# An S4 convolution and gated MLP on one core: the opening's pole tables, w_mod and x loads, and the reads of x at the convolution's end

## Chip, cores and metric

The kernel runs on one core of a Trainium2 chip. The metric is the device time of one execution in microseconds (us), as the median over runs. PE is TensorE's matmul stream, DVE is VectorE, ACT is ScalarE, POOL is GpSimd, SP is SyncE; SP and POOL issue most DMAs, each from a queue of its own.

## The reference

x is 2048 positions by 576 channels, split by the kernel into 16 blocks of 128 positions.

```python
mod = (silu(c) @ w_mod).reshape(1, 6, 1, -1)     # sa, ca, ga, sb, cb, gb; w_mod is 576 x 3456
h = layernorm(x) * (1 + ca) + sa
# S4: dt = exp(log_dt); K[d,l] = Re sum_n C[d,n] exp(dt (A_re + i A_im) l) dt B[d,n]
x = x + ga * (causal_conv(h, K) + h * Dskip)      # by rfft/irfft of length 4096
h = layernorm(x) * (1 + cb) + sb
z = gelu(h @ w_in)                                # 576 x 4608
g = w_sp @ layernorm(z[..., 2304:]) + b_sp        # w_sp is 2048 x 2048
out = x + gb * ((z[..., :2304] * g) @ w_out)
```

## The kernel before

**Stages.** The first stage builds the convolution's kernel K for 36 groups of 16 channels, layer-normalises x, and convolves; it ends with the first MLP operations near 385 us of the profile. The rest is the MLP. The change touches the first stage, and the loads for the MLP that this stage starts.

**The opening.** `poles` turns log_dt, A and B*C (576 x 128 poles) into three tables: the real exponent and log weight (`al`, `lw`), the turns of one and of 64 positions (`tau`, `tau64`), and a phase `ph`. It runs as p0 for the first quarter of the channels (tiles 128x144) and as p1 for the other three (128x432). `split3` cuts each table into three bf16 parts (copy on ScalarE, subtract on VectorE, twice), which GpSimd's queue writes to DRAM (`pa_d`, `pb_d`, rows of 288 bytes). `poles_load` reads them back, turned, as `lb`, `lc` and `la`; from there TensorE with `sel` makes exponents and angles. A unit e copies and exponentiates the exponents into a tile `et` (ScalarE), a unit t takes sine and cosine into `ft` (VectorE rounds, ScalarE evaluates), a unit p multiplies both (VectorE, tiles `pg`, 1024 wide) and k and 1 contract them on TensorE.

**Modulation and normalisation.** `mod_load` brings one sixth of w_mod (two tiles of 648 KB; tiles `wm`, or for k=0,1 the buffers named k_a and k_b, which hold K later). `mod_unit` multiplies it by silu(c) on TensorE into psum tiles `pk`, copies them to `mpart` (ScalarE), sums over partitions, and makes `gar` (from 2), `cga` (from 1) and `sga` (from 0). `ln_load` brings four blocks of x (1152 KB), `ln_stats` takes mean and variance: with two passes of ScalarE for the first two fours, with VectorE's batch-norm statistics for the rest. `ln_rows` scales a block by `cga` (VectorE) and makes a small row tile `rt`.

**The convolution's end.** Units u, z and v transform and multiply; v is copied from psum by ScalarE and written to DRAM (`v_d`) by GpSimd's queue. `y_vload` reads v_d in another layout, `y_xload` a block of x, a unit y adds both on TensorE and ScalarE or VectorE and stores x1. Steps L are the MLP's start: loads of w_in quarters into `wst` (L0: the third, 1.31 MB), their sums of squares on ScalarE (`start_sum`), scales, and the high and low f16 parts (`start_hi`, `start_lo`) into `wz`. Then the first rows of x1 are normalised (`xz`, `n`), transposed (`pt`, `nt`) and multiplied (`pz`).

**What sets the order.** ORDER is a list written out by hand: each token runs the next piece of one unit, and engines execute in that program order. O and P are p0 and p1, M, S, R, A are mod_unit, ln_stats, ln_rows, ln_half; w and i load w_mod on SyncE's or GpSimd's queue, x and j load x, r, g and a load r1t, Q is poles_load. PLAN lists, for each ring of buffers, which buffer each new tile takes; buffer letters (et_a, pk_b) are those of the ring. Nearly every instruction is recorded at the helper's line 224.

Of the kernel before, what the change touches and what calls it, by code (L numbers as in the profile page):

```python
# [18 lines left out]
D = 576  # L19
# [13 lines left out]
    "et": "0123401232013423014021304123024104120",  # L33
# [21 lines left out]
B0 O0 O0 O0 O0 B2 O0 O0 O0 O0 B7 O0 B1 O0 O0 O0 B6 O0 O0 O0 O0 O0 O0 x0 O0 O0 O0 O0 P0 S0 O0 S0 B3 O0 O0 i2 O0 O0 O0 P0 M2 O0 O0 S0 S0 B4 P0 S0 O0 Q0 P0 e1 S0 M2 e1 i1 e0  # L55
P0 P0 g0 e1 e0 P0 e0 e1 P0 t1 t2 i0 g1 O0 M2 e0 P0 M1 t1 t2 t1 P0 P0 t0 w3 P0 M1 t0 M2 t1 t0 t2 M1 M0 M1 M0 t0 e2 j1 R1 P0 p1 M3 t2 M0 p1 M3 R0 e2 R3 e6 p1 M0 B5 e2 M0 e6
M3 w4 k1 e4 e2 P0 M3 k1 O0 P0 e3 11 p0 e4 11 e6 M4 M0 e5 p0 P0 p0 e6 S1 S1 p2 M4 k0 M4 p2 11 R2 p2 e5 k0 e5 S1 M0 M3 M0 P0 k2 M4 e5 M0 P0 t5 k2 A0 e3 A0 S1 A0 A0 A0 w5 t5
S1 e3 P0 e3 A0 t3 S1 A1 t5 A1 A1 r2 A1 P0 t3 R4 A1 t7 A0 R5 A1 A2 A2 O0 P0 t3 t3 A2 A2 t4 P0 A1 A2 A2 A3 p3 A2 A3 t5 P0 r3 A3 A3 t4 t4 j2 M4 10 10 e4 A3 A3 A3 e4 12 p3 12
e7 p3 e7 P0 e7 R7 t7 10 R6 P0 p5 S2 12 k3 e8 e7 O0 k3 e8 A4 S2 A4 S2 A4 e8 S2 A4 A4 A4 e8 p5 P0 A5 t4 A5 A5 P0 A5 p5 A5 p4 A5 t7 a4 A4 A5 t6 A6 A6 A6 p4 A6 t6 A6 p4 A6 t8
A7 A7 P0 t7 A7 A7 O0 k4 A6 P0 S2 A7 13 t6 p7 A7 k4 t8 p7 R9 14 13 O0 k5 P0 P0 a5 t6 14 14 t8 p7 Q1 13 t8 M5 x3 k7 P0 e11 R8 A7 k5 M5 S3 k7 S3 A8 A8 e11 R11 e9 A8 e10 e11  # L60
P0 e9 e11 P0 p6 S3 S3 A8 P0 A8 R10 t10 A8 e10 A9 t10 A9 A9 A9 p8 p8 r6 e10 A9 A9 t9 e10 t10 A10 A8 P0 A10 A10 A10 A9 t11 p6 A10 A10 17 P0 t10 M5 p6 17 k6 M5 p8 t11 t9 17
k6 A11 A11 r7 S3 t11 t11 e12 A11 A11 Q2 15 R13 A11 A11 A10 p11 k8 t9 15 15 R12 A11 k8 A12 p11 A12 e12 A12 p11 A12 e14 A12 t14 A12 A13 e14 p10 A13 t14 A13 R15 e9 p10 A13
p10 A13 R14 A13 e9 t14 A12 e12 t12 e12 A14 A14 t9 A14 t15 A14 A14 t12 A13 t14 A14 t12 A15 A15 t14 O0 O0 A15 e16 k10 P0 A15 P0 A15 16 A15 P0 O0 p9 t12 k11 16 M5 p9 A14 A15
p9 C0 16 t14 18 c1 k10 f0 18 110 k11 18 110 e14 U2 110 U1 U0 t15 p12 111 t15 111 z2 111 t15 u2 t16 p12 u2 U5 p12 u0 e14 k9 c0 z2 z2 u0 k9 t16 k12 U4 p14 u1 19 U14 t16 U7
e16 k12 e15 19 t16 19 U23 e13 e15 e15 e16 u1 e15 c3 u7 e16 e13 p14 u4 u7 e13 u4 p14 c2 p15 z1 z1 e13 t13 U29 v2 u14 U6 t16 v2 p15 z4 U10 u14 t13 u6 t13 p15 t18 k15 z4 u6
u5 t16 k15 z1 p16 t18 p16 u29 e18 u5 U15 v1 z0 t13 u29 t18 e17 X1 t18 v1 U3 e18 115 115 u10 v1 v2 z0 u10 z0 X3 p16 e17 115 k14 k14 u3 b1 e17 e22 u3 p13 U12 e22 t17 e17
# [20 lines left out]
def consts():  # L87
# [53 lines left out]
    rgt = np.zeros((6, 8, 8, 32))  # L141
    rge = np.zeros((6, 8, 8, 32))
    rpe = np.zeros((6, 8, 8, 64))
    rgt[:3] = eye[None, :, :, None] * a
    rgt[3:] = eye[None, :, :, None]
    rge[:3] = eye[None, :, :, None] * (64 * a)
    rge[3:] = eye[None, :, :, None]
# [89 lines left out]
def ssm(tc, I, x1_d, consts_s, dram, mod_d, mlp):  # L237
# [6 lines left out]
    with ExitStack() as ctx:  # L244
# [26 lines left out]


        def poles(c0, c1, Q, own=None):
            w = 144 * (c1 - c0)
            f0, f1 = CW * c0, CW * c1

            def t(n, dt=F32):
# [2190 lines left out]
```

## Time and profile before

| | |
|---|---|
| three runs | 1690.81, 1693.52, 1693.48 us; median 1693.48 |
| profiled execution's own time | 1691.0 us |
| its span | 1688.9 us |
| busy PE / DVE / ACT / POOL | 1615.6 / 1298.4 / 873.8 / 209.7 us |
| 200 to 300 us, busy PE / DVE / ACT | 96.98 / 97.85 / 95.52 us |
| first p unit (pg_a) | 51.29 us |
| last y unit's matmuls end, first transposes of n begin | 383.85, 384.32 us |
| granted TensorE clock | 0.99 |

A row of the timeline gives start, duration, engine, line, operation, out<-in, shape and count; the bracket at its end is the idle time just before it, with what ended that. In tables by window the columns are busy time and instructions of each engine, then clock, share of the 16 DMA engines and GB/s.

### The profile page before, as it was taken

The numbers are of one execution on the slowest core, as the hardware profiler recorded it, in microseconds if no ns is written. First come the engines' busy times: TensorE is split into PE (matmuls) and PEld (weight loads), VectorE is DVE, ScalarE is ACT, GpSimd is POOL, SyncE is SP. The second block draws the span as 40 slices with busy tenths as digits, with TensorE's granted clock in tenths as the row PEclk, the third lists the DMA queues.
The fourth block names the chain that finished last, engine by engine and source line by source line (L and its number), as shares of the span: only waits on it lengthen the run. The fifth ranks groups of instructions, "written<-read, shape, count | busy, mean of one in ns | idle before, by whom it ended". The sixth has DMA issues, their size and how long they took to land.

```text
span 1688.9 us, 39922 instructions
## 1 busy us (share of the span) xinstructions
PE 1615.6 (96%) x16868; PEld 1235.7 (73%) x16868; DVE 1298.4 (77%) x2241; ACT 873.8 (52%) x1307; POOL 209.7 (12%) x340
## 2 busy tenths in 40 slices
PE   3778999989999999999999999999999999999999
PEld 1344677755555557778878888888888888888887
DVE  7898999867989877988997776894443487787555
ACT  6889999675776664555444433342321133353221
POOL 3251111112222110000000000000111100111100
PEclk9978999999999999999999999999999999999999
DMA  9667645596888898776738887664667573777560
GB/s 231 170 215 229 203 140 176 171 317 208 280 287 243 251 261 297 242 270 234 249 118 302 282 292 257 219 218 166 232 213 243 189 221 121 275 281 252 189 241 29
DMA packets 186402, 380.61 MB, mean 225 GB/s; under 512 B 38464, under 2 KB 105792, under 8 KB 185456
## 3 DMA queue, kind: packets, MB, share of 16 engines
q1 hardware_dynamic: 145216, 182.10, 35.2%
q0 software_dynamic: 34528, 169.11, 30.1%
q10 hardware_dynamic: 6480, 26.86, 3.9%
q8 instruction: 132, 2.16, 0.5%
q14 instruction: 46, 0.38, 0.1%
HBM read 272.73 MB, written 105.29 MB: 224 GB/s over the span
## 4 chain that ended last, share of the span: by engine, by line
PE 77%; DVE 7%; DMA 3%; issue 2%; ACT 2%; SPq 0%; POOL 0%; ACTq 0%; DVEq 0%; POOLq 0%
PE ps L224 58%; PE pz L224 10%; PE pk_b L224 2%; PE pk_a L224 2%; DMA zset<-set_d 2%; PE pk_c L224 2%; PE pk_d L224 1%; DVE zset L224 1%; DVE gt L224 1%; DVE bsz L224 1%; PE ps_a L224 0%; PE ps_b L224 0%; DMA v_d<-v_a 0%; PE pt L224 0%; DMA uu_a<-in_x 0%
## 5 line engine op out<-in xcount | busy, mean ns | idle before, releaser
L224 PEld LDWEIGHTS <-zset 128*128 128x128 f16 x7182 | 702.2, 98 | 86.5 <-DMA zset<-set_d 2.0
L224 PE MATMUL ps<-wsp,zset 128*128 128x256 f16 x6048 | 666.8, 273 | 2.2 <-DMA zset<-set_d 1.1
L224 PE MATMUL pz<-wz,nt 128*128 128x512 f16 (+1 forms) x1120 | 220.8, 358 | 1.5 <-ACT nt L224 1.0
L224 ACT ACTIVATE z<-gt 128x1024 f16<-128x1024 f32 x56 | 59.0, 1054 | 250.4 <-DVE gt L224 250.4
L224 PEld LDWEIGHTS <-nt 128*128 128x128 f16 x1120 | 109.4, 98 | 107.1 <-ACT nt L224 1.5
L2164 POOL DMA_DIRECT2D zset<-set_d x96 | 50.8, 529 | 862.5 <-PE ps L224 619.7
L224 PE MATMUL ps<-wout,z 128*128 128x288 f16 x1092 | 138.4, 286 | 0.0
L224 DVE SCALAR_TENSOR_TENSOR gt<-ps,sc,bsp 128x512 f32<-128x512 f32 x36 | 27.0, 749 | 143.0 <-PE ps L224 141.3
L224 PEld LDWEIGHTS <-z 128*128 128x128 f16 x1176 | 115.1, 98 | 28.9
L224 DVE TENSOR_TENSOR raw<-raw 128x256 f32<-128x256 f32 (+3 forms) x238 | 126.8, 539 | 7.7 <-DMA raw<-z_d 3.5
L224 PE MATMUL ps<-n2o,zset 128*128 128x256 f16 x1134 | 128.2, 273 | 0.0
L224 DVE SCALAR_TENSOR_TENSOR gt<-ps,sc,gt 128x512 f32<-128x512 f32 (+1 forms) x180 | 122.2, 696 | 7.6
L224 ACT ACTIVATE zset<-raw 128x1792 f16<-128x1792 f32 x48 | 81.1, 1691 | 59.3 <-PE ps L224 21.6
L224 DVE TENSOR_TENSOR zset<-raw,zset 128x1792 f16<-128x1792 f32 x48 | 96.9, 2020 | 15.7 <-ACT zset L224 15.7
L224 DVE TENSOR_TENSOR z<-ps,z 128x512 f32<-128x512 f32 (+1 forms) x126 | 72.0, 599 | 32.3 <-ACT z L224 25.9
L224 ACT ACTIVATE z<-pz,sc 128x512 f32<-128x512 f32 (+1 forms) x96 | 51.9, 574 | 39.9 <-PE pz L224 32.7
L224 ACT ACTIVATE wsp<-raw,sc 128x1792 f16<-128x1792 f32 x25 | 44.5, 1783 | 46.2 <-DVE raw L224 40.2
L224 ACT ACTIVATE z<-z,sc 128x1024 f32<-128x1024 f32 x21 | 24.1, 1148 | 76.0 <-DVE z L224 72.3
L224 ACT ACTIVATE z1b<-gt 128x512 f16<-128x512 f32 (+1 forms) x22 | 17.7, 821 | 84.0 <-DVE gt L224 84.0
L224 PE MATMUL ps<-n2q,wf 128*128 128x512 f16 x252 | 55.7, 379 | 0.0
L224 DVE BATCH_NORM_STATS2 bsz<-z 128x6 f32<-128x384 f32 x96 | 48.4, 548 | 5.0 <-ACT z L224 4.4
L224 DVE SCALAR_TENSOR_TENSOR wsp<-raw,sc,wsp 128x1792 f16<-128x1792 f32 x25 | 52.0, 2078 | 0.3 <-ACT wsp L224 0.3
(793 smaller groups left out, 2772.0 us busy)
## 6 DMA issues: line engine op xcount, KB each, us to landing
zset<-set_d POOLq DMA_DIRECT2D x96, 896.0 KB, 5.2
raw<-z_d SPq DMA_DIRECT2D x48, 512.0 KB, 5.6
set_d<-zset ACTq DMA_DIRECT2D x24, 896.0 KB, 6.4
z_d<-z POOLq DMA_DIRECT2D x32, 576.0 KB, 8.2
zset<-wa_d POOLq DMA_DIRECT2D x18, 896.0 KB, 4.9
raw<-in_w_spT SPq DMA_DIRECT2D x25, 512.0 KB, 4.4
set_d<-zset SPq DMA_DIRECT2D x12, 896.0 KB, 5.8
wst<-in_w_in SPq DMA_DIRECT2D x8, 1024.0 KB, 9.3
```

Source lines behind the costliest of these rows:

```text
L224: return self.tc.keep_in_program_order(f(*a, **k))
L2164: self.nc.gpsimd.dma_start(o, self.set_d[f, j - 1] if j else self.wa_d[f])
```

## The change

- **Pole tables.** `poles` returns ten separate chains that ORDER steps one by one. The four products of B and C are one instruction, both absolute values one, `tau64` needs no multiplication (the factor 64 stands in a constant), the angle takes 8 operations where it took 13, and `split3` works on two tables at once. All parts go to one DRAM tensor `p_d`. A_re is loaded last. p0's tiles lie in two buffers of the et ring.
- **Loads.** w_mod 2, 1, 0, r1t 0 and 1, and x blocks 4 to 7 are issued by SyncE right behind `small`. GpSimd's queue keeps the pole tables; the two memsets of `lb` run first.
- **Statistics.** The second four blocks of x use VectorE's batch-norm statistics. `rt` is made for two blocks at once.
- **The convolution's end.** A tile `xl` holds x blocks 8 to 15 for channels 384 to 575; it is loaded with `x1l` (now four blocks) at step D, and three loads of x in steps X fall away. The third quarter of w_in is loaded ahead of some dozen other loads of SyncE that it stood behind, into the unused half of a k1 buffer and a new tile `wrow`; its sum of squares is two instructions, and the sum of the fourth quarter moves behind the last v copies. Step L14 moves behind a piece of y9, and the last y pieces change places.

Some of the code (`...` marks what is left out; the rest of ORDER and PLAN is in the rows below):

```diff
-        def poles(c0, c1, Q, own=None):
+        def poles(c0, c1, Q, order, own=None):
...
-                V.tensor_tensor(wr, Cr, Br, op=ALU.mult)
-                V.tensor_tensor(wi, Ci, Br, op=ALU.mult)
-                V.tensor_tensor(q1, Ci, Bi, op=ALU.mult)
...
+                V.tensor_tensor(s(10, 4).rearrange("p (b c f) -> p b c f", b=2, c=2), bc(sm(6, 2)[:, None], shape), bc(sm(8, 2)[:, :, None], shape), op=ALU.mult)
...
+            def split3(i, m, row, at):
...
+                A.activation(pt[:, :, 0], src, AF.Copy)
+                yield
+                V.tensor_tensor(q, src, pt[:, :, 0], op=ALU.subtract)
...
+            return [step(), turns(), weights(), log(), ratio(), second(), angle(),
+                    split3(1, 2, 6, 0), split3(3, 2, 0, 2), split3(5, 1, 12, 4)]
...
-            if i < 2:
+            if i < 1:
...
-            elif c == NC - 1:
-                xb = mlp.x1l[:, 4 * q - 4:4 * q]
+            elif (c, q) == (NC - 1, 1):
+                xb = mlp.x1l
+            elif c >= NC - 2 and q > 1:
+                xb = mlp.xl[:, 4 * q - 8:4 * q - 4, CH0[c] - 384:CH0[c] - 384 + CHW[c]]
...
-        self.x1l = wzp.tile([128, 12, CHL], F32, name="x1l")
-        S.dma_start(self.x1l, I["x"][:, 4:, D - CHL:])
+        self.x1l = wzp.tile([128, 4, CHL], F32, name="x1l")
+        S.dma_start(self.x1l, I["x"][:, 4:8, D - CHL:])
+        self.xl = wzp.tile([128, 8, D - 384], F32, name="xl")
+        S.dma_start(self.xl, I["x"][:, 8:, 384:])
...
+    def start_early(self, q, pool, t):
+        self.wts[q] = t, pool.tile([128, 512], F32, name="wrow", bufs=1)
+        self.win_parts(*self.wts[q], FH + 512 * q, 512)
```

GpSimd's queue in the opening, before: pole writes, a load of w_mod among them, then the three reads and more loads.

```order
L224 DMA pb_d<-pt 64x3x144 x2
L224 DMA pa_d<-pt 64x3x144 x4
L224 DMA pb_d<-pt 64x3x144 x2
L224 DMA wm<-in_w_mod 96x1728 x2
L224 DMA pa_d<-pt 64x3x144 x2
L224 MEMSET lb 32x1152
L224 DMA lb<-pb_d 48x1152 x2
L224 DMA lc<-pa_d 48x1152 x2
L224 DMA la<-pa_d 48x1152 x2
L224 DMA k_a<-in_w_mod 96x1728 x2
```

The same queue after the change.

```order
L223 MEMSET lb_124 32x1152
L223 MEMSET lb_126 32x1152
L223 DMA p_d<-pt 64x6x144 x2
L223 DMA lc<-p_d 48x1152 x2
L223 DMA p_d<-pt 64x6x144 x2
L223 DMA p_d<-pt 64x3x144 x2
L223 DMA lb_124<-p_d 48x1152 x2
L223 DMA la<-p_d 48x1152 x2
L223 DMA p_d<-pt 64x6x144 x12
```

The read of `lc` moved ahead of the writes of (`al`, `lw`) and of `ph`; the loads of w_mod left this queue.

VectorE on p0's weights B*C, before: from the first product to the multiplication by the reciprocal.

```order
L224 TENSOR_TENSOR t_wr<-et_a 128x144
L224 TENSOR_TENSOR t_wi<-et_a 128x144
L224 TENSOR_TENSOR t_q_126<-et_a 128x144
L224 TENSOR_TENSOR t_wr<-t_wr,t_q_126 128x144
L224 TENSOR_TENSOR t_q_127<-et_a 128x144
L224 TENSOR_TENSOR t_wi<-t_wi,t_q_127 128x144
L224 TENSOR_SCALAR et_a<-t_wr 128x144
L224 TENSOR_SCALAR et_a<-t_wi 128x144
L224 TENSOR_TENSOR et_a<-et_a 128x144 x2
L224 TENSOR_SCALAR et_a<-et_a 128x144
L224 RECIPROCAL t_rnd<-et_a 128x144
L224 TENSOR_TENSOR et_a<-et_a,t_rnd 128x144
```

The same place after; the second row is the first subtraction of `split3`, the three of `ec` belong to silu(c).

```order
L223 TENSOR_TENSOR et_e<-et_a 128x576
L223 TENSOR_TENSOR et_e<-et_a,pt 128x288
L223 TENSOR_SCALAR ec<-ec 96x6
L223 RECIPROCAL ec<-ec 96x6
L223 TENSOR_TENSOR ec<-ec,cT 96x6
L223 TENSOR_TENSOR et_e<-et_e 128x144 x2
L223 TENSOR_SCALAR et_a<-et_e 128x288
L223 SCALAR_TENSOR_TENSOR et_a<-et_a 128x144
L223 TENSOR_TENSOR et_a<-et_a 128x144
L223 RECIPROCAL et_e<-et_a 128x144
L223 TENSOR_TENSOR et_a<-et_a,et_e 128x144
```

Thirteen instructions of the weights became eight, of up to four times the width.

ScalarE near 350 us, before: the last copies of v (to v_a and v_b) around the sums of squares of the third and fourth quarters of w_in.

```order
L224 ACTIVATE v_a<-pk_d 128x256
L224 ACTIVATE v_a<-pk_b 128x256
L224 ACTIVATE wz,acc<-wst 128x5x512 x2
L224 ACTIVATE v_b<-pk_d 128x256
L224 ACTIVATE v_b<-pk_b 128x256
L224 ACTIVATE v_a<-pk_c 128x256
L224 ACTIVATE v_a<-pk_a 128x256
L224 ACT_TABLE_LOAD
```

And after.

```order
L223 ACTIVATE v_a<-pk_d 128x256
L223 ACTIVATE v_a<-pk_b 128x256
L223 ACTIVATE wz,acc<-k_a 128x4x512
L223 ACTIVATE wz,acc<-wrow 128x512
L223 ACTIVATE v_b<-pk_d 128x256
L223 ACTIVATE v_b<-pk_b 128x256
L223 ACTIVATE v_a<-pk_c 128x256
L223 ACTIVATE v_a<-pk_a 128x256
L223 ACTIVATE wz,acc<-wst 128x5x512
L223 ACT_TABLE_LOAD
```

One of the two sums moved behind the last v copies, and the other reads the buffer that is loaded earlier.

More of the change, by code (lines that the diff above doesn't have):

```diff
@@ L384, in run @@
-                for part in (second, angle) if own is not None else (angle, second):
-                    yield from part()
-                yield from split3((ph, pa_d, 6))
-            return run()
-        lt = {}
-        def poles_load(c, Q):
-            for n, d_, k in (("lb", pb_d, 0), ("lc", pa_d, 0), ("la", pa_d, 3)):
-                t_ = tb.tile([112, 9, 128], BF, name=n)
-                if n == "lb":
-                    Q.memset(t_[32:64], 0.0)
+                V.scalar_tensor_tensor(ph, ax, -math.pi / 2, ph, op0=ALU.mult, op1=ALU.add)
@@ new lines, in angle @@
+                V.scalar_tensor_tensor(ph, tau, 31.5, ph, op0=ALU.mult, op1=ALU.add)
+                yield
+            def split3(i, m, row, at):
+                if own is None or not pt0:
+                    pt0[:] = [eb.tile([128, 2592], BF, name="pt", bufs=1)]
+                at = 0 if own is None else 3 * w * at
+                pt = pt0[0][:, at:at + 3 * w * m].rearrange("p (m q f) -> p m q f", m=m, q=3)
+                src, q = sm(i, m), sm(15, m)
+                A.activation(pt[:, :, 0], src, AF.Copy)
+                yield
+                V.tensor_tensor(q, src, pt[:, :, 0], op=ALU.subtract)
+                yield
+                A.activation(pt[:, :, 1], q, AF.Copy)
+                yield
+                V.tensor_tensor(pt[:, :, 2], q, pt[:, :, 1], op=ALU.subtract)
+                yield
+                pq = pt.rearrange("p m q f -> p (m q) f")
+                for c in range(c0, c1):
+                    for h in range(2):
+                        Q.dma_start(p_d[c, h, row:row + 3 * m].rearrange("q (p f) -> p q f", p=64),
+                                    pq[64 * h:64 * h + 64, :, 144 * (c - c0):144 * (c - c0) + 144])
+                yield
@@ L528, in ssm @@
         row = {}
+        rts = {}
         def ln_rows(b):
@@ L831, in begin @@
                 S.dma_start(dsk, I["dsk"])
-            else:
-                mod_init()
+            elif n == 7:
+                mod_init()
+            else:
+                for i in range(2):
+                    lbs.append(tb.tile([112, 9, 128], BF, name="lb%d" % i, bufs=1))
+                    G.memset(lbs[i][32:64], 0.0)
         def middle(n):
@@ L988, in win_scales @@
         ps = self.ps1()
-        nc.tensor.matmul(ps[:, :2], self.ones, self.acc[:, q:q + 2], start=True, stop=True)
+        nc.tensor.matmul(ps[:, :2], self.ones, self.acc[:, q:q + 2], start=True, stop=q != 7)
+        if q == 7:
+            nc.tensor.matmul(ps[:, :1], self.ones, self.acc[:, 80:81], start=False, stop=True)
         V.tensor_copy(cols(N_W), ps[:, :2])
```

259 lines of the change are left out of this document (121 added, 138 removed).

## The prediction

> **What bounds the kernel now.** I read the page for the shares, then the table by windows for the places where TensorE is not full, then the timeline of each engine there, with its waits. Busy time of each engine on the page, and five stretches of the table (columns: length, busy PE, PEld, DVE, ACT, POOL with counts, clock, DMA share, GB/s):
>
> ```profile
> PE 1615.6 (96%) x16868; PEld 1235.7 (73%) x16868; DVE 1298.4 (77%) x2241; ACT 873.8 (52%) x1307; POOL 209.7 (12%) x340
> ```
>
> ```profile
> 40.00:50.00 10.00, 8.52 (x44) 3.43 (x48) 3.34 (x6) 5.84 (x11) 0.53 (x1) 1.00 1.01 267
> 200.00:300.00 100.00, 96.98 (x2256) 71.38 (x2254) 97.85 (x128) 95.52 (x166) 13.54 (x23) 1.00 0.55 164
> 320.00:330.00 10.00, 10.00 (x253) 7.86 (x252) 9.63 (x11) 3.53 (x9) 1.08 (x2) 1.00 0.33 108
> ...
> 350.00:390.00 40.00, 31.58 (x323) 19.86 (x322) 24.08 (x58) 22.21 (x32) 11.44 (x17) 1.00 1.02 286
> ```
>
> TensorE is busy for 96% over all; behind 390 us the change alters no instruction's order, so I carry whatever shift stands there to the end. What can move lies in front: an opening in which VectorE does 3.34 us of work in ten while the DMA engines are at 1.01; a middle, 200 to 300, in which VectorE (97.85) and ScalarE (95.52) are both full, so that an earlier start passes through it one for one; and the convolution's end, 350 to 390, with 8.42 us of idle TensorE at a DMA share of 1.02. The stretch before, 320 to 330, has DMA to spare (0.33).
>
> **The opening: when the tables arrive.** The end of p0's weights on VectorE, GpSimd's queue, and how long its DMAs take to land (columns of the third: KB each, median us from issue to landing):
>
> ```profile
> 8.92 0.31 DVE L224 TENSOR_TENSOR et_a<-et_a,t_rnd 128x144 f32<-128x144 f32 x1
> ```
>
> ```profile
> 13.21 1.43 POOL L224 DMA_DIRECT2D pb_d<-pt  x2 [12.75 <-DVE pt L224]
> ...
> 20.44 0.55 POOL L224 DMA_DIRECT2D wm<-in_w_mod  x1 [2.10 <-DMA pb_d<-pt]
> ...
> 25.58 1.03 POOL L224 DMA_DIRECT2D lb<-pb_d  x2 [0.29 <-POOL lb L224]
> ...
> 28.78 0.99 POOL L224 DMA_DIRECT2D la<-pa_d  x2 [1.19 <-DMA pa_d<-pt]
> ```
>
> ```profile
> k_a<-in_w_mod POOLq DMA_DIRECT2D x1, 648.0 KB, 10.2
> ...
> pa_d<-pt POOLq DMA_DIRECT2D x6, 54.0 KB, 5.5
> ...
> lb<-pb_d POOLq DMA_DIRECT2D x2, 108.0 KB, 3.4
> ```
>
> Before, the read of `lb` is issued at 25.58, behind two loads of w_mod, the phase and a memset. After, that queue holds pole data alone, but in series: write the turns, wait for their landing to read `lc`, write (al, lw) and the phase, wait again, read `lb`. The turns' last subtraction stands behind the product with the reciprocal, which ended at 9.23 before, in a chain of about that length: I put the first write near 10.4, where it was 13.21. With 5.5 per landing `lc` is issued at 16 to 17; the writes behind it take until 19.5 and land near 24.5; `lb` is issued at about 25 and lands, at 3.4 to 5.5, between 28 and 31. I take 30 for the first matmul of a unit e. That is no gain: the shorter arithmetic is eaten by the second wait. The ends are 27 (each landing 1.5 shorter) and 34.
>
> What follows on ScalarE and TensorE:
>
> ```profile
> 22.74 0.78 ACT L224 ACTIVATE st1o_a<-ln_x,nm 128x576 f32<-128x576 f32 x1 [1.33 <-DVE nm L224]
> ...
> 30.74 1.02 ACT L224 ACTIVATE et_b<-ps_a 128x1024 f32<-128x1024 f32 x1
> ...
> 32.57 0.61 ACT L224 ACTIVATE et_b<-pk_c 128x512 f32<-128x512 f32 x1
> ...
> 33.68 1.28 ACT L224 ACT_TABLE_LOAD   x1
> ```
>
> ```profile
> 30.09 0.61 PE L224 MATMUL ps_a<-sel,lb 48*128 48x512 bf16 x2
> ...
> 43.61 2.13 PE L224 MATMUL pk_d<-k_a,ec 96*32 96x288 f32 x12 [1.39 <-DMA k_a<-in_w_mod]
> ...
> 49.72 1.29 PE L224 MATMUL pk_a<-k_b,ec 96*32 96x288 f32 x10
> ```
>
> ```profile
> 47.61 1.22 DVE L224 TENSOR_SCALAR ft_c<-ps_a 128x1024 int32<-128x1024 int32 x1 [4.54 <-PE ps_a L224]
> ...
> 51.12 0.25 DVE L224 TENSOR_SCALAR rt<-r1t,r 128x64 f32<-128x64 f32 x1
> 51.29 2.35 DVE L224 TENSOR_TENSOR pg_a<-et_b,ft_a 128x1024 f32<-128x1024 f32 x2
> 57.28 1.11 DVE L224 TENSOR_TENSOR pt<-t_sq,pt 128x432 bf16<-128x432 f32 x2
> 58.31 1.22 DVE L224 TENSOR_TENSOR pg_b<-et_c,ft_c 128x1024 f32<-128x1024 f32 x1
> ...
> 105.19 0.60 DVE L224 TENSOR_TENSOR pt<-t_sq,pt 128x432 bf16<-128x432 f32 x1
> ```
>
> Before, M1 waits for w_mod at 43.61, VectorE 4.54 us behind it, and the first p unit starts at 51.29. After, w_mod 2 and 1 stand early in SyncE's queue and that wait goes. But ScalarE now does in one run: three e units (three of 1.02 and three of 0.61, some 4.2 in steps), the four squares of x (0.78 and 0.19 for reading each sum, 3.6), p1's logarithms and arctangent with two table loads (2 x 1.28 and about 2), a pair of splits, `mpart`: 14.5 us from 30 to 44.5. Then table, two sines, two cosines, `gar`, `mpart` (7 us), the sums over partitions and `cga`: pg_a near **54.5**, 3.2 later than before. With `lb` at 27 it is 52, with 34 it is 58.5.
>
> TensorE's price in that run depends on its speed: twelve w_mod matmuls take 2.13 at 43.61, ten take 1.29 at 49.72, both with the granted clock at 1.00; I took 2.13. The Trainium skill ("TensorE: Matmul & The Clock Gate", Part 1) says that the array runs at half rate until a window of some 3.4 us has been busy. The trace's two speeds agree in kind, though the clock column doesn't show it. By it M1, close behind other matmuls, could cost about 0.6 less for each of its halves, and pg_a would come some 1.2 earlier.
>
> **The opening: what is left to do after pg_a.** Further rows:
>
> ```profile
> 53.17 1.00 ACT L224 ACTIVATE pt<-t_sq 128x432 bf16<-128x432 f32 x2
> ...
> 62.59 0.67 ACT L224 ACTIVATE st1o_b<-ln_x 128x576 f32<-128x576 f32 x1
> ...
> 71.52 0.77 ACT L224 ACTIVATE st1o_b<-ln_x,nm 128x576 f32<-128x576 f32 x1
> ```
>
> ```profile
> 93.31 0.82 DVE L224 BATCH_NORM_STATS2 bs<-ln_x 128x6 f32<-128x288 f32 x2 [0.36 <-DMA ln_x<-in_x]
> ...
> 152.04 2.36 DVE L224 TENSOR_TENSOR pg_b<-et_b,ft_b 128x1024 f32<-128x1024 f32 x2 [4.47 <-PE pk_c L224]
> ```
>
> VectorE: from the first to the last quoted pt row, 23 instructions of p1 stand behind pg_a (the first pair takes 1.11, the last one 0.60); counted from start to start, 0.52 for most, they take 12.35. After the change four are left (two 864 wide, two 432): from 0.52 at 432 and 1.13 at 1024 the 864-wide is about 0.97, together 3.0. That is 9.3 less. The statistics of the second four of x come to VectorE: four times (0.82 + 0.21), with steps 3.6 more. `rt` saves half of its sixteen 0.25 us rows, some 0.5 because the new ones are twice as wide; one `ln_x` row that stood ahead of pg_a stands behind it, 0.7 more. Sum: 9.3 - 3.6 + 0.5 - 0.7 = **5.5 less**. The batch-norm price is the trace's own; the merged 864-wide ones are bounded by 0.6 (as the 432) and 1.22 (as the 1024), which moves the sum by under 1.
>
> ScalarE: two passes over four blocks, 3.1 + 3.34 = 6.4, go; the third e unit (1.4) was done earlier; split copies 1.1: **9.1 less**.
>
> At 152.04 VectorE waits 4.47 for a contraction, which ran late behind a ScalarE without gaps. So VectorE arrives there at 147.57 + 3.2 - 5.5 = 145.3, and ScalarE's chain at 152.04 + 3.2 - 9.1 = 146.1. The later one counts: the opening is worth 5.9; since full engines seldom keep every microsecond, I take **5**. Ends: pg_a at 52 gives 8.4 (9.5 with a faster TensorE), pg_a at 58.5 gives 2; beyond that it turns to a loss.
>
> **The convolution's end.** ScalarE, TensorE and the two queues:
>
> ```profile
> 354.06 2.34 ACT L224 ACTIVATE wz<-wst 128x2560 f16<-128x2560 f32 x1 [2.74 <-DMA wst<-in_w_in]
> ...
> 358.71 0.36 ACT L224 ACTIVATE v_b<-pk_d 128x256 f32<-128x256 f32 x1
> ```
>
> ```profile
> 359.13 0.38 PE L224 MATMUL pk_d<-acc,ones 128*128 128x2 f32 x2 [2.77 <-ACT v_b L224]
> 375.02 1.10 PE L224 MATMUL pk_c<-uu_h,small 128*128 128x512 f32 x2 [1.10 <-DMA uu_h<-in_x]
> 379.23 1.10 PE L224 MATMUL pk_b<-uu_a,small 128*128 128x512 f32 x2 [2.09 <-DMA uu_a<-in_x]
> 384.32 0.76 PE L224 MATMUL pt<-ident,n 128*128 128x128 f32 x5 [0.48 <-ACT x1l L224]
> ```
>
> ```profile
> 340.32 3.39 SPq L224 DMA_DIRECT2D wst<-in_w_in  x3
> ...
> 375.68 2.40 SPq L224 DMA_DIRECT2D uu_d<-v_d  x2
> ```
>
> ```profile
> uu_d<-v_d SPq DMA_DIRECT2D x2, 128.0 KB, 4.3
> ```
>
> Before, ScalarE waits 2.74 for the w_in quarter that SyncE issues at 340.32 into full DMA engines, does two sums, and only then copies the last v, for which TensorE stands 2.77; the v writes on GpSimd's queue, the v reads and the last y units follow. After, that quarter is loaded where the DMA share is 0.33, the wait goes, and one sum (2.3) stands ahead of the copies: they come at about 354 at the earliest, but TensorE ends the last v only at 356.4 (359.13 - 2.77), so copies and writes come 2.8 earlier. Then the waits of 1.10 and 2.09 for x go with the loads, since `xl` is loaded near 333 us; SyncE issues two less ahead of the last v reads. 2.8 + 1.1 + 2.1 = 6.0, less what the next limit keeps: the last v read is the last of four pairs, which SyncE issues in some 2 us each from 364 on (uu_d took 2.40), and lands 4.3 later, near 377, so pt comes at about 378.5 instead of 384.32. I take **5.5**. `xl` adds 786 KB near 333, `x1l` loses 262 KB: 0.52 MB at the 286 GB/s of the last window is 1.8 us of DMA time, in a stretch that loses 1.31 MB. Ends: 8.0 (TensorE's whole idle time, 8.42, but for 0.5), and 2 if the v writes land late and the 2.8 alone is kept.
>
> **The sum.** 5 + 5.5 = 10.5 from the profiled execution's 1691.0 gives 1680.5. That execution is 2.5 below the median 1693.48; two of three runs are at the higher value, so I put 1 us back: **1681.5**.
>
> **The rivals.** (1) Only the convolution's end gains: `lb` at about 35, pg_a 8 later, eats all the 5.9. 1691 - 5.5 = 1685.5. For it: three round trips at 5.5 in series. Against: they already stand in my sum. (2) Only the opening gains, because the last v reads land no earlier at a DMA share above 1: 1686. Against: 1.31 MB leave that stretch. (3) Neither gains, say VectorE, with statistics added, is late at 100 us, and the end is bound by v_d: about 1691. (4) Slower, by one mechanism: the pole tables starve. SyncE's queue now holds six tiles of w_mod in one run (4.0 MB, 15 us at the 267 GB/s of 40 to 50) and x behind them, while three pole trips in series go through GpSimd's. If each lands like k_a's load, 10.2 instead of 5.5, `lb` comes 14 later, at 44; above 40.5 the loss exceeds both gains, one for one: 1691 + 3.5, up to 1700. For it: the engines stand at 1.01 there. Against: small pole DMAs landed in 5.5 in the same crowd, so I give it little. The Trainium skill ("DMA: Bandwidth & Descriptors", Queues, rings and completion order) says that an engine takes turns between the queues that have work, a packet at a time. By that a short queue isn't stuck behind a long one, and the 5.5 beside the loads' 10.2 agrees. (5) All terms at their good ends: 1691 - 8.4 - 8 = 1674.6.
>
> **How the numbers follow.** Forecast (1676 to 1684) 0.55; (1) 0.15; (2) 0.10; (3) 0.08; (4) 0.07; (5) 0.05. The range 1673 to 1692 leaves out (4) and a part of (3) and (5). A change of under 0.2% (3.4 us) can't be told from none: faster means below 1690.1, slower above 1696.9. Faster: the forecast, (1), (2) and (5), 0.85; within 0.2%: (3), 0.08; slower: 0.07.
>
> **What would show it.** In the opening: `lb`'s first matmul near 30, no wait for k_a, pg_a at 54 to 55, and at the contraction that stands at 152.04 now a time near 147, with VectorE's wait there below 2. At the end: no wait for wst ahead of the v copies, those some 8 us earlier in all (5 of them from the opening), no PE wait for a load of x, and pt at 384.32 - 5 - 5.5. A pole read landing past 35, or v_d's reads landing 6 us behind their issue, would make it wrong.

## The result and the profile after

| | before | after |
|---|---|---|
| median of 5 runs, us | 1693.52 | 1723.00 |
| range | 1690.81 to 1703.07 | 1720.36 to 1723.89 |
| span of the profiled execution | 1688.9 | 1721.2 |

The change makes the kernel slower by 1.6%: the ratio is 1.0159, with a 95% interval of 1.0138 to 1.018. Fewer instructions are left on VectorE, ScalarE and GpSimd, as the page of the kernel after says:

```profile
PE 1621.2 (94%) x16870; PEld 1242.1 (72%) x16870; DVE 1295.3 (75%) x2212; ACT 870.2 (51%) x1285; POOL 193.7 (11%) x311
```

The opening first. These are GpSimd's queue, the DMAs issued in the first 30 us (KB each, median us to landing), and the matmul that waits for the second half of `lb`, the first copy of its result on ScalarE, VectorE's next operation and the first p unit.

```profile
10.26 1.48 POOL L223 DMA_DIRECT2D p_d<-pt  x2 [7.47 <-DVE pt L223]
17.98 1.45 POOL L223 DMA_DIRECT2D lc<-p_d  x2 [6.24 <-DMA p_d<-pt]
19.43 2.57 POOL L223 DMA_DIRECT2D p_d<-pt  x4
29.52 0.53 POOL L223 DMA_DIRECT2D lb<-p_d  x1 [7.52 <-DMA p_d<-pt]
```

```profile
k_b<-in_w_mod SPq DMA_DIRECT2D x2, 648.0 KB, 21.6
...
p_d<-pt POOLq DMA_DIRECT2D x4, 108.0 KB, 8.5
...
p_d<-pt POOLq DMA_DIRECT2D x2, 54.0 KB, 10.3
lb<-p_d POOLq DMA_DIRECT2D x1, 108.0 KB, 8.1
```

```profile
39.26 0.60 PE L223 MATMUL ps_a<-sel,lb 48*128 48x512 bf16 x1 [0.95 <-DMA lb<-p_d]
...
39.90 1.02 ACT L223 ACTIVATE et_b<-ps_a 128x1024 f32<-128x1024 f32 x1 [19.46 <-PE ps_a L223]
...
44.28 1.22 DVE L223 TENSOR_SCALAR ft_a<-ps_b 128x1024 int32<-128x1024 int32 x1 [16.73 <-ACT et_d L223]
...
62.71 2.35 DVE L223 TENSOR_TENSOR pg_a<-et_b,ft_a 128x1024 f32<-128x1024 f32 x2
```

The first write goes out at 10.26, near the 10.4 of the forecast. Then the DMAs of the three trips land after 8.1 to 10.3 us (each row gives a median) where 5.5 and 3.4 were reckoned with. ScalarE stands idle for 19.46 us and VectorE for 16.73, and the first p unit starts at 62.71.

The next two fences are the table by windows, the kernel before and then the kernel after, over the stretch from the first p unit to the 15th copy of v or u on ScalarE (columns as in the prediction).

```profile
51.29:184.36 133.07, 107.99 (x2350) 60.95 (x2342) 122.95 (x209) 125.42 (x238) 42.30 (x66) 0.87 0.66 200
```

```profile
62.71:206.76 144.05, 114.92 (x2361) 66.24 (x2355) 118.51 (x195) 117.14 (x214) 29.20 (x46) 0.83 0.60 180
```

VectorE has 4.4 us less to do and ScalarE 8.3 less, nearly the 5.5 and 9.1 of the forecast, and yet the stretch is 11 us longer.

At the convolution's end, ScalarE's timeline of before and after, and the landing of the v writes in the 20 us or so around, before and after:

```profile
316.07 0.38 ACT L224 ACTIVATE v_b<-pk_a 128x256 f32<-128x256 f32 x1 [0.15 <-ACT ft_a L224]
```

```profile
343.33 0.39 ACT L223 ACTIVATE v_b<-pk_a 128x256 f32<-128x256 f32 x1 [3.06 <-DMA v_d<-v_b]
```

```profile
v_d<-v_b POOLq DMA_DIRECT2D x3, 256.0 KB, 3.6
```

```profile
v_d<-v_b POOLq DMA_DIRECT2D x2, 256.0 KB, 5.9
```

The waits for wst and for x are gone, but the quarter of w_in that is now loaded near 332 lands beside the v writes: these take 5.9 us instead of 3.6 (medians of two and three DMAs; 5.3 in e8_endfix below, which has the same load), and ScalarE's next copy waits 3.06 for one of them. The last copies of v, which in before waited 2.74 us for that quarter, now wait for a v write:

```profile
382.98 0.38 ACT L223 ACTIVATE v_b<-pk_d 128x256 f32<-128x256 f32 x1 [2.21 <-DMA v_d<-v_b]
```

And in the MLP, SyncE's queue, GpSimd's and TensorE after, and SyncE's queue before (z is written to DRAM and read back into `raw`; `wf` holds weights read from DRAM):

```profile
644.15 0.91 SPq L223 DMA_DIRECT2D raw<-z_d  x2
```

```profile
644.25 1.01 POOL L223 DMA_DIRECT2D z_d<-z  x1 [7.73 <-ACT z L223]
```

```profile
656.48 4.57 PE L223 MATMUL ps<-n2q,wf 128*128 128x512 f16 x14 [7.79 <-DMA wf<-win_d]
```

```profile
607.05 0.94 SPq L224 DMA_DIRECT2D raw<-z_d  x2
```

The read of z that in before is issued at 607.05 is now issued at the time of GpSimd's write of a later z, which waits for ScalarE. That the read waits for ScalarE too is taken from these times; the profile names no releaser. The load of `wf` behind it on SyncE is late, and TensorE waits 7.79 us. No instruction was moved here. `xl` makes its SBUF pool 4 KB per partition larger than before, and so moves the pools behind it.

### The profile page after: what moved, and what is told of

It is laid out like the page before. It is cut to its first block, busy times and chain, and to the rows that moved or that the text cites. A ratio compares the mean times of both kernels' runs of the same rounds, so it can differ in the third digit from the quotient of the medians.

```text
span 1721.2 us, 39837 instructions
## 1 busy us (share of the span) xinstructions
PE 1621.2 (94%) x16870; PEld 1242.1 (72%) x16870; DVE 1295.3 (75%) x2212; ACT 870.2 (51%) x1285; POOL 193.7 (11%) x311
```

## The experiments

Every profile is cut at three marks: the first p unit, the 15th copy of v or u on ScalarE, and the first transposition behind the convolution (384.32 before). The table gives the times, and for the stretch between the first two marks TensorE's busy and idle time in it. Each kernel has one profile, so a position in the table carries the scatter of a single execution.

| kernel | us | ratio, 95% interval | first p unit | 15th copy | TensorE busy + idle | copy to transposition | to the end |
|---|---|---|---|---|---|---|---|
| before | 1693.52 | | 51.29 | 184.36 | 107.99 + 25.08 | 199.96 | 1304.58 |
| after | 1723.00 | 1.0159, 1.0138 to 1.018 | 62.71 | 206.76 | 114.92 + 29.13 | 200.33 | 1314.11 |
| e1_end | 1702.46 | 1.0041, 1.0029 to 1.0053 | 50.76 | 186.65 | 110.25 + 25.64 | 197.77 | 1314.68 |
| e2_open | 1717.34 | 1.013, 1.0104 to 1.0155 | 65.72 | 210.50 | 114.01 + 30.77 | 204.15 | 1305.35 |
| e3_loads | 1713.77 | 1.0108, 1.0093 to 1.0123 | 53.38 | 197.73 | 114.43 + 29.92 | 198.73 | 1313.74 |
| e4_pad | 1705.08 | 1.0054, 1.0033 to 1.0075 | 46.83 | 187.78 | 116.24 + 24.71 | 203.61 | 1312.81 |
| e5_loads | 1700.35 | 1.0034, 1.0018 to 1.005 | 53.49 | 191.34 | 114.98 + 22.87 | 200.23 | 1307.23 |
| e6_stats | 1696.88 | 1.0018, 1.0004 to 1.0033 | 47.19 | 189.75 | 110.42 + 32.14 | 201.81 | 1304.94 |
| e7_poles | 1699.38 | 1.0037, 1.0024 to 1.005 | 50.00 | 193.96 | 116.64 + 27.32 | 200.66 | 1303.58 |
| e8_endfix | 1693.05 | 1.0000, 0.9988 to 1.0011 | 47.26 | 187.81 | 113.95 + 26.60 | 198.58 | 1305.61 |
| e9_fix | 1719.47 | 1.0146, 1.0129 to 1.0164 | 64.81 | 209.50 | 115.35 + 29.34 | 200.00 | 1308.60 |
| e10_late | 1708.84 | 1.0087, 1.0065 to 1.0108 | 54.75 | 200.60 | 116.20 + 29.65 | 199.78 | 1305.52 |
| e11_statsback | 1706.86 | 1.0069, 1.0047 to 1.009 | 53.98 | 198.80 | 117.36 + 27.46 | 200.02 | 1306.48 |
| e15_m4late | 1696.79 | 1.0012, 0.9997 to 1.0026 | 49.48 | 187.82 | 112.98 + 25.36 | 201.94 | 1304.64 |
| e16_m4early | 1706.63 | 1.0068, 1.0046 to 1.0089 | 54.45 | 196.06 | 112.45 + 29.16 | 198.88 | 1306.46 |
| e17_best | 1705.54 | 1.0068, 1.0047 to 1.0088 | 55.10 | 202.03 | 115.91 + 31.02 | 199.37 | 1305.50 |
| e18_psum | 1702.71 | 1.0056, 1.0039 to 1.0073 | 54.36 | 196.03 | 113.45 + 28.22 | 198.37 | 1304.60 |

Four of these profiles have before's opening, instruction for instruction: before, e1_end, e4_pad and e8_endfix. Their 15th copy comes at 184.36 to 187.81, on average at 186.7, and before's is the earliest; I compare with the average. A difference of 3 us at one profile's copy is no more than these four differ among themselves.

### The two halves of the change, and the pools

e1_end is the kernel before with the last part of the change's diff alone, the reads at the convolution's end; e2_open is it with all the rest of the diff, the opening.

> The kernel before with the change's last part alone (late loads of x replaced by xl, the third quarter of w_in loaded early, the order of the end); the opening is that of before. Theory A (the end does what was predicted, but the first read of z_d in the second MLP phase now waits for ScalarE, because xl moves the pools behind it by 4 KB): the transposes of n come 4 to 6 us earlier than at 384.32, a TensorE wait of 7 to 8 us for wf appears in the MLP, total 1695 to 1698 against 1693.5. Rival B (the end itself gains nothing, and the wait in the MLP comes from the late opening): transposes near 384, no wait for wf, total 1692 to 1695.

> The change's opening alone (pole tables, loads, statistics, order up to the convolution's end), with the convolution's end of before. Theory A: lb lands near 38 to 40, the first p unit at 62 to 63, the loss grows to 22 to 24 us by 170 us and is carried to the end: total 1716 to 1719, no wait for wf. Rival B (the wait for wf is part of the late opening): 1723 to 1725, with that wait.

The end alone makes the kernel slower by 0.41%, although its way from the 15th copy to the transposition is shorter (197.77 us against 199.96); behind that, 1314.68 us stand where before has 1304.58, with a TensorE wait of 7.13 for `wf`. That is the wait of theory A, but the transposition stays at 384.42, and the time is above its range. The opening alone costs 1.3% and has no such wait: theory A for its time, with a first p unit 3 us later than expected. e4_pad adds nothing but an unused tile:

```diff
         self.x1l = wzp.tile([128, 12, CHL], F32, name="x1l")
+        wzp.tile([128, 1024], F32, name="pad")
```

> The kernel before, with an unused tile of 4 KB per partition in the pool that holds x1l, and nothing else. Theory A (the shift of the pools behind it makes the first read of z_d share memory with a tile that ScalarE still writes): a TensorE wait for wf of 5 to 8 us near 630 us and total 1698 to 1702. Rival B (the added wait costs nothing by itself, only in a kernel that is late): 1693 to 1695.

It costs 0.54%, and the last column of the table shows where: 1312.81. TensorE's wait is there too:

```profile
639.20 3.17 PE L224 MATMUL ps<-n2q,wf 128*128 128x512 f16 x7 [6.21 <-DMA wf<-win_d]
```

That is theory A, at a price above its range. e8_endfix has the change's end, with the tile of x for the channels 384 to 511 in a pool of its own, which is closed with the convolution, and the rest of it in `x1l` as before:

```diff
-        self.xl = wzp.tile([128, 8, D - 384], F32, name="xl")
+            mlp.xl = mlp.pool(ctx, "xlp", 1).tile([128, 8, 128], F32, name="xl")
```

> The kernel before, with the change's convolution end alone, and the 4 KB tile of x that the change adds put where it doesn't move the pools that the gated output and the MLP use. Theory A (the end's new reads gain their 4 to 5 us, and the moved pools took them back through the late load of wf): no wait of TensorE for wf of 6 to 8 us near 640, time 0.15 to 0.3% below before. Theory B (the end gains nothing, and the loss of the first experiment is not the pools'): time at before's or above, though the wait for wf is gone.

The wait for `wf` is gone and the last part takes 1305.61, as theory A has it, but the time is that of before, as theory B has it. So the end's gain is small. From the copy to the transposition it is 201.8 us on average in the seven kernels of the table with before's end (199.96 to 204.15) and 199.2 in the ten with the new one (197.77 to 200.33). That is some 2.6 us, against 5.5 in the forecast, and in the time not even this is seen: the interval of e8_endfix (0.9988 to 1.0011) allows 2 us at most. e9_fix takes the pools out of the change itself.

> The kernel after, with only the 4 KB tile of x put where it doesn't move the pools of the gated output and the MLP. Theory A (the moved pools make the first read of z for the MLP wait for ScalarE and VectorE, so the loads of wf behind it come late): no wait of TensorE for wf near 650, the time from the first transposition behind the convolution to the end 8 to 9 us shorter than in the kernel after (about 1305 in place of 1314.1), 1713 to 1715 us beside a before of 1694. Theory B (the wait for wf is a sign, not the cost): that stretch stays above 1312 us.

The first read of z is free again, 12 us earlier than in the kernel after although e9_fix's opening happens to be 2.7 us later, and TensorE runs on without a wait for `wf` (SyncE's queue of e9_fix, then TensorE's):

```profile
632.03 0.91 SPq L223 DMA_DIRECT2D raw<-z_d  x2
```

```profile
640.66 15.27 PE L223 MATMUL ps<-n2q,wf 128*128 128x512 f16 x70
```

The last part falls by 5.5 us, to 1308.60, less than the 8 to 9 expected. The time falls by 3.5, and the intervals of the two ratios overlap: in the change itself the size of this cost is uncertain. Its presence isn't: in the last column the four kernels with the larger pool stand apart from all others, and only they wait for `wf` (6.21 to 7.79 us).

### The loads of the opening

e3_loads is the change with w_mod, r1t and the second x tile back behind the pole tables; e5_loads is the kernel before with only these loads moved.

```diff
-B3 B4 w2 w1 w0 r0 r1 x1 B6 B5 O1 ... O8 O9 O9 ... q1 q2 P2
+B3 B4 B6 B5 O1 ... O8 i2 O9 O9 ... q1 q2 i1 g0 i0 g1 j1 P2
```

> The changed kernel, but w_mod 2, 1, 0, r1t 0 and 1 and the second four blocks of x are issued by GpSimd's queue behind the pole reads, as before the change. Theory A (the pole tables' three round trips are starved by those loads, and the 11 us that the loss grows by behind the first p unit come from the late start): p_d and lc land in 4 to 6 us instead of 6 to 10, lb's first matmul at 28 to 31, the first p unit at 52 to 56, total 1698 to 1703. Rival B (the start is repaired, but the new order of units is slower by itself behind it): first p unit at 52 to 56 and total 1709 to 1714. Rival C (the round trips are slow whatever else is loaded): lb near 38, total 1720 or more.

> The kernel before, with only the loads of the opening moved: w_mod's six tiles, r1t and the x tile of the second statistics run in one row on SyncE's queue, as the change has them; the pole code, the order of the arithmetic and the convolution's end are those of before. Theory A (the long SyncE queue starves the pole trips, and that sets the opening): the pole write lands in 7 to 9 us where it took 5.5, the read of lb in 8 where it took 3.4, so the first matmul of a unit e comes at 35 to 38 us instead of 30.1, the first p unit 4 to 6 us later than 51.3, the time 0.3 to 0.6% above before. Theory B (the moved loads do no harm by themselves; the order of the new pole code, fed late, does): the first p unit within 2 us of before, the time within 0.2%.

In e5_loads the DMAs issued by 32 us show the starving by itself (before: 5.5, 5.8 and 3.4):

```profile
pa_d<-pt POOLq DMA_DIRECT2D x6, 54.0 KB, 9.2
pb_d<-pt POOLq DMA_DIRECT2D x4, 54.0 KB, 9.5
lb<-pb_d POOLq DMA_DIRECT2D x2, 108.0 KB, 9.1
```

The first matmul on `lb` moves to 36.51, the first p unit to 53.49 (49.0 on average with before's opening), the 15th copy comes 4.7 us late and the time rises by 0.34%: theory A. The moved loads stand in another queue and are also issued earlier; no run separates the two. In e3_loads the tables land after 2.4 to 7.1 us, and TensorE and VectorE start where the prediction put them (28.17 and 53.38 against 30 and 54.5):

```profile
28.17 0.68 PE L226 MATMUL ps_a<-sel,lb 48*128 48x512 bf16 x2 [28.17 <-DMA lb<-p_d]
```

But the kernel stays slower than before by 1.08%: rival B. The starving costs the change about 9 us at the 15th copy (206.76 against 197.73) and 0.5% of the time; another 11 us (197.73 against 186.7) stand there without it.

### The parts of the opening, one at a time

e6_stats takes only the statistics to VectorE; e7_poles takes only the new functions for the pole tables, their steps laid at the places of before's (the tokens O and P of ORDER).

```diff
-            if i < 2:
+            if i < 1:
```

> The kernel before, with one part of the change: the statistics of the second four blocks of x on VectorE (batch-norm statistics) in place of ScalarE's two passes over each. Theory A (ScalarE is the fuller engine of the opening, VectorE has room): ScalarE loses about 6.4 us and VectorE gains 4.1 in front of 100 us; time 0.1 to 0.3% below before. Theory B (VectorE bounds the stretch from the first p unit to 153 us, 93.0 of 101.9 us busy, so whatever it gains there is paid by the end): time 0.2 to 0.3% above before (3.6 to 4.1 us of 1695). Theory C (that stretch is not bound by one engine's work): within 0.15% either way.

> The kernel before, with the new code for the pole tables alone (its chains laid at the places where before has its own; loads, statistics and the convolution's end as before). Theory A (fewer operations are worth what they save: 9 us less VectorE work behind the first p unit): the time 0.2 to 0.5% below before. Theory B (the stretch up to 170 us is set by the row of matmul, sine, product and copy, each waiting for the one before, and not by how much work an engine has): within 0.2% of before. Theory C (the table's trip through DRAM, two in series where before had one ahead of lb, costs more than the arithmetic saves): first p unit 3 us or more later, time 0.2 to 0.4% above.

The statistics cost 0.18% (interval 0.04 to 0.33%), nearest to theory B: the 4.1 us more on VectorE, as reckoned ahead, are not made up by the 6.4 less on ScalarE. In this profile TensorE's idle time is 32.14 us, the highest of the table. The pole code costs 0.37%, though VectorE has less to do, and the 15th copy comes 7.3 us late. That is the time of theory C, but not for its reason, since the first p unit, at 50.00, is not 3 us late. One wait in it is new (ScalarE's timeline):

```profile
86.91 0.92 ACT L223 ACTIVATE pt<-e 128x864 bf16<-128x864 f32 x1 [4.79 <-DMA p_d<-pt]
```

There is one buffer `pt` for the two-table splits, and here the next split waits until the last one's write has landed. Neither the kernel after nor e3_loads has this wait of ScalarE for `p_d`, since their splits stand elsewhere in the order. So e7_poles doesn't show what the pole code costs in the change.

### Why the stretch behind the first p unit stays long

The row of e3_loads, and a wait in it on VectorE:

```profile
53.38:197.73 144.35, 114.43 (x2361) 64.89 (x2355) 118.68 (x195) 116.61 (x214) 29.13 (x46) 0.83 0.60 180
```

```profile
74.22 1.06 DVE L226 TENSOR_TENSOR pt<-e,pt 128x864 bf16<-128x864 f32 x1 [3.38 <-ACT pt L226]
```

From here on the tile of x lies as in e8_endfix. e10_late moves that subtraction behind three blocks of statistics; e11_statsback takes the statistics back to ScalarE, and e12_both does both.

```diff
-... e3 e5 t5 P8 e3 k2 M0 A0 A0 P8 t5 S1 ... A0 S1 A1 S1 A1
+... e3 e5 t5 e3 k2 M0 A0 A0 t5 S1 ... A0 S1 P8 A1 S1 P8 A1
```

> The kernel of e3_loads (the change with the opening's loads on their old queues) with the tile of x as in e8_endfix, and the second subtraction and the writes of p1's second split moved behind three of the four blocks of statistics in the written order. In e3_loads VectorE waited there 3.38 us for ScalarE's copy, which stood behind other copies. Theory A (the stretch behind the first p unit is set by such waits in the written order): the wait goes, the 15th copy of v or u comes at 194.5 to 195 us in place of 197.7, and the time is 1701 to 1703 us. Theory B (something behind it binds, so that one wait less is one more later): that copy within 1 us of 197.7, the time 1704 to 1706 us, as e3_loads less the pools' 8 to 9.

> The kernel of e3_loads with the tile of x as in e8_endfix, and the statistics of the second four blocks of x back on ScalarE, at the places that they had in the kernel before. Theory A (VectorE's 4.1 us more are paid for, as in e6_stats, ScalarE's 6.4 less are not used): the 15th copy of v or u 3 to 4 us earlier than 197.7, time 1701 to 1703 us. Theory B (in the new order both engines wait more than they work, so that neither side of the trade matters): within 1.5 us of 197.7, 1704 to 1706 us. Theory C (ScalarE is what the new order waits for): later than 199, above 1706 us.

> The kernel of e11_statsback with the later second subtraction of e10_late. What is left of the change against the kernel before is the new pole code in its own order and the convolution's end. If the two causes add up, the 15th copy of v or u comes at 190 to 192 us and the time is 1697 to 1699 us; if they cover the same idle time, at about 194.5 and 1701 us; if neither counts, at 197.7 and 1705 us.

In e10_late the wait is gone, yet no kernel of the three gained: the 15th copy comes at 200.60 and 198.80, no earlier than in e3_loads. That is nearest to theory B, though the times, 1708.84 and 1706.86, lie above its range, and e10_late's copy is 2.9 us from 197.7, where it allows 1. e12_both took 1710.77 (ratio 1.0088, 1.0064 to 1.0111), more than any of its three cases; it has no profile that can be used.

Then I suspected the one unit of w_mod, M4, that the change moves from near 62 us to near 93 (its matmuls in before and in e3_loads). The rows show the part of ORDER where it arrives; of its places in before, one is in them.

```diff
-... t4 t4 j2 M4 10 10 ... t7 10 R6 P0 p5 S2 12 k3
+... t4 t4 j2 10 10 ... t7 10 R6 M4 P0 p5 w5 S2 12 M4 k3
```

> The kernel before, with one thing moved: the fifth unit of w_mod (M4: twelve matmuls, two copies, the sums over partitions, two copies, one write) and the load of the sixth tile behind it stand where the change has them, between the units of x near 100 us instead of near 65; nothing else differs. In the kernels with the change's order the writes of u fall behind by 4 to 6 us between the third and the fifth of them, which is where M4 now stands. Theory A (that place is where the stretch behind the first p unit loses its time: TensorE's and ScalarE's queues do M4 there while the row of x units waits): the fifth write of u 4 to 5 us later against the third than in the kernel before, the 15th copy of v or u at 190 to 192 us (186.7 as the mean of the four profiles with before's opening), time 0.2 to 0.3% above before. Theory B (M4 is no matter, the new pole code's waits are): within 1.5 us there and within 0.1% in time.

> The kernel of e3_loads with the tile of x as in e8_endfix, and M3 and M4 put back to the places beside the p units that they have in the kernel before (M3 right behind the first p unit, M4 where the change has M3). Theory A: the fifth write of u 11 to 12 us behind the third (15.7 in e3_loads), the 15th copy of v or u at 192 to 194 us instead of 197.7, time 1700 to 1702 us. Theory B: the stretch keeps its 144 us, 1704 to 1706 us.

Both seemed to bear it out: 1698.77 (1.0034, 1.0019 to 1.005) with a 15th copy at 191.51, and 1697.63 (1.0032, 1.0019 to 1.0045) with one at 189.07. But a few sums in PSUM (one place in e13_m4late, five in e14_m4early) are written over there before they are read, so neither kernel computes the same sums, and their times decide nothing. e15_m4late and e16_m4early do the same with free buffers (for e16_m4early, the order of the change against its own):

```diff
-p1 M0 M0 p1 p1 R1 M0 e6 R0 w3 ... R2 M3 p2 P8 e5 k0 p2 M3 w4 e3
+w3 ... p1 M0 M0 p1 p1 R1 M0 M3 w4 e6 R0 M3 ... R2 M3 M4 p2 P8 e5 k0 p2 M4 e3
```

> As e13_m4late (the kernel before with M4 and the load behind it at the change's places), with PSUM buffers for M4 that are free there, so that the output is whole; e13_m4late overwrote sums that were still to be read. Theory A: as there, the fifth write of u some 15 to 18 us behind the third instead of 11, time 0.2 to 0.35% above before. Theory B (what e13_m4late showed came from the buffers): 11 to 12 us, time within 0.1% of before.

> As e14_m4early (the change with its loads on the old queues, the tile of x out of the way, and M3 and M4 beside the p units), with PSUM buffers that are free there. Theory A: the fifth write of u 10.5 to 12 us behind the third, the stretch from the first p unit to the 15th copy of v or u 135 to 138 us instead of 144 to 146, time 1696 to 1699 us. Theory B: 144 us and 1704 to 1706 us.

> The kernel of e16_m4early with the statistics of the second four blocks of x on ScalarE again. Of the change are left the new pole code, its place in the order and the convolution's end; loads, statistics, pools and the fifth unit of w_mod stand as before. If the statistics cost here what they cost in e6_stats, 3 us: 1693 to 1696 us, level with before. If the new order takes them for nothing, as in e11_statsback: as e16_m4early.

This is theory B for e15_m4late, 1.0012 with an interval that holds 1, and near it for e16_m4early, 1706.63 us with the 15th copy at 196.06, 1.7 us before e3_loads, which is within the scatter of single profiles. Its stretch of 141.61 us lies between the two theories. The suspicion fell. e17_best, e16_m4early with the statistics on ScalarE, is no faster either (1705.54). e18_psum gives 17 of the sums other free buffers (`PLAN["pk"]`), for the case that the choice of buffers counts:

> The kernel of e16_m4early with another choice of PSUM buffers for 17 of the sums between the fourth and the eighth unit of x: those that the kernel before uses there, and another free one at the two places where they are still to be read. Order, loads and instructions are those of e16_m4early. Theory C (the choice of buffers that goes with the change's order makes TensorE and ScalarE wait for each other there; e13_m4late took the change's choice into the kernel before and lost, e14_m4early took before's choice into the change and gained): the fifth write of u 10.5 to 12 us behind the third (14.2 in e16_m4early), the stretch 136 to 138 us, time 1697 to 1700 us. Theory D (e14_m4early gained because five of its sums were written over before they were read, so that waits were gone): 141 to 145 us, time 1704 to 1708 us.

The copy comes at 196.03, as in e16_m4early, so theory C fell; the time, 1702.71, lies between the two ranges. Theory D is left, but the trace doesn't show it. In e14_m4early's stretch

```profile
53.57:189.07 135.50, 105.68 (x2359) 61.53 (x2351) 118.13 (x195) 116.14 (x215) 29.25 (x46) 0.90 0.64 192
```

TensorE waits for 29.82 us, no less than the 29.16 of e16_m4early. The stretch is shorter by TensorE's busy time (105.68 against 112.45 us), at a granted clock of 0.90, and this execution, at 1694.41 us, is the fastest of nine. Why the nine are faster stays open.

The table of windows tells what is common to all these. The rows of e8_endfix (before's opening) and e16_m4early (the change's):

```profile
47.26:187.81 140.55, 113.95 (x2354) 63.82 (x2354) 123.59 (x209) 125.91 (x239) 42.31 (x66) 0.83 0.65 196
```

```profile
54.45:196.06 141.61, 112.45 (x2359) 65.32 (x2351) 118.51 (x195) 116.17 (x214) 29.18 (x46) 0.82 0.60 184
```

Subtract TensorE's busy time from the length. In the four profiles with before's opening 24.7 to 26.6 us are left, though their lengths differ by 8 us. With the change's opening and the tables on time (e3_loads, e10_late, e11_statsback, e16 to e18) 27.5 to 31.0 are left, 29.2 on average. So the new order makes TensorE wait 3.7 us longer, with less work on VectorE and ScalarE. The rest of the length is TensorE's busy time. For the same instructions it goes with the granted clock: 107.99 us at 0.87, 110.25 at 0.85, 113.95 at 0.83, 116.24 at 0.82.

Work on another engine can still matter: e6_stats, before's order with 3 us more busy time on VectorE in this stretch, leaves 32.14. But in the new order, taking the statistics back did not shorten the waits both times: it left 27.46 in e11_statsback and 31.02 in e17_best.

Which waits make up the 3.7 stays open: taken singly, the subtraction, the statistics, M4 and the choice of PSUM buffers do not. Two places stand out in the traces and were not tried (TensorE in e3_loads):

```profile
57.22 0.75 PE L226 MATMUL pk_b<-mpart,small 128*128 128x288 f32 x2 [2.12 <-ACT mpart L226]
```

```profile
119.47 0.29 PE L226 MATMUL pk_b<-dsk,small 128*32 128x4 f32 x8 [5.31 <-issue]
```

The first wait is 2.12 us in all six kernels and at most 1.29 in any kernel of the table with before's order. The second, in front of one contraction near 120 us, is 2.99 to 5.31 in the six and at most 1.23 in the others. Together they are more than 3.7, so other waits became shorter; that they are the cause is not shown.

## Why the prediction was wrong

- **The pole trips.** The first write and the order of the trips were right; the size of each landing was not: 8.5 to 10.3 for the writes where I had 5.5, 8.1 for `lb` where I had 3.4 to 5.5. That puts the first full set of matmuls at 39.26, where I had 30. It is the mechanism of my rival (4), to which I gave 0.07, in a milder form: by my own sum a loss begins only above 40.5, so this step alone doesn't make the kernel slower. I set it aside because small DMAs had landed in 5.5 "in the same crowd". They had, but then the six w_mod tiles stood in GpSimd's own queue, between and behind the pole tables; e5_loads moves these loads and nothing else, to the other queue and to an earlier time, and the same DMAs take 9.2 to 9.5. The rule that I weighed there, of the Trainium skill ("DMA: Bandwidth & Descriptors", Queues, rings and completion order), that an engine takes turns between the queues with work, is no promise of a short landing: beside the long queue `lb` took 9.1 us in e5_loads, beside the short one 3.4.
- **What is left to do after the first p unit.** This step failed in kind. The instructions that go were counted well, but I took the saved work as saved time because both engines are nearly full behind it (97.85 and 95.52 of 100 us). (ScalarE's terms add up to 8.9, not 9.1; that moves the sum by 0.2.) With the tables on time (e3_loads: first p unit at 53.38) the 15th copy should have come earlier than in before and came 11 us later than the average of before's opening. Of the 11.9 us in the six kernels named above, 5.3 are the first p unit (54.3 against an average of 49.0, of which before's profile, at 51.29, hid 2.3), 3.7 are more waits of TensorE, and 2.9 a longer busy time (115.0 against 112.1), which is within the spread of before's own four profiles (108.0 to 116.2). So the wait of TensorE took the place of the gain that I had booked; its cause stays open.
- **The clock.** I reckoned with one profile. Its clock in that stretch, 0.87, is the highest of the kernels in the table, and its span of 1688.9 is 5.0 below what the averages of the three parts make (186.7 + 201.8 + 1305.4).
- **The convolution's end.** The waits that I named went. In their place the v writes beside the moved load of w_in take 5.9 us, and the last v copies wait 2.21 for one, nearly as long as before for w_in (2.74). Of the 5.5, 2.6 are left in the profiles, near the lower end of 2 that I had kept for v writes landing late, and none is seen in the time of e8_endfix. That the v writes cost the difference is argued, not tested.
- **"Whatever shift stands there to the end."** No instruction moved behind 390 us, but the pools did: 8.5 us on average in the four kernels with the larger pool (1312.8 to 1314.7) against the others (1305.4, e9_fix, at 1308.60, aside). I had looked at instructions and DMAs and not at where the buffers lie.

In sum, the kernel after against these averages: 20.1 us lost at the 15th copy (some 9 by starved tables, 11 of which only the place is known), 1.5 gained between copy and transposition, 8.7 lost behind it, 27.3 us; the medians differ by 29.5.

## What to carry to other kernels

An order of loads that takes work off a queue can starve a chain of small DMAs in series on it: add up the trips at the landing time of the new crowd, not of the old one. In a stretch where several engines hand work to each other, look at the waits of the engine whose busy time and idle time make up the length (here TensorE), and don't book another engine's saved work as time without a run. A tile that grows moves every pool behind it: compare the waits of later stages as well, and look at more than one profile of the kernel before.

## What the runs showed of the hardware

- The same instructions took 108.0 to 116.2 us of TensorE's time in the same stretch, at a granted clock of 0.87 to 0.82, so that two executions that began it 4 us earlier (46.83 and 47.26 against 51.29 and 50.76) ended it later.
- The DMAs of the pole tables, 54 and 108 KB on GpSimd's queue, landed in 9.1 to 10.6 us beside six w_mod tiles (3.9 MB) issued early on SyncE's queue (e5_loads), and in 3.3 to 5.8 with these tiles later and on the pole tables' own queue (before).
- An unused tile of 4 KB per partition in one SBUF pool cost 0.54%. The part behind the convolution took 1312.81 us against 1305.4 on average, with TensorE waiting 6.21 us for a load 639 us into the kernel. That one DMA waits there for a buffer's new neighbours is inferred from the times.
